# A convolution and a SiLU layer on one core: third product with x kept by token halves, and a new order with one run of each stage a block

## Chip, cores, metric

One core of one Trainium2 chip runs the whole program. The metric is device time in microseconds (us) of that core, the median of the runs shown; 2227.32 us for the kernel before (three runs, 2227.03 to 2227.95).

## What is computed

The reference, cut to what matters. A causal convolution with 7 taps along the tokens (24 channels share one set of taps, which come from a softmax), then two matrix products with SiLU between them, in fp32:

```
w = softmax(weight)                                  # [8 heads, 7 taps]
x_unf = x_pad[:, idx, :].reshape(B, S, K, H, group)  # x: [8, 4096, 192]
x = np.einsum('hk,bskhg->bshg', w, x_unf).reshape(32768, 192)
h = x @ w_in                                         # w_in: [192, 2048]
g = h * (1.0 / (1.0 + np.exp(-h)))
out = g @ w_out                                      # w_out: [2048, 192]
```

## The kernel before

The 32768 tokens go in 32 blocks (NB) of 1024 tokens (TT), each made of two halves of 512 (TB). The weights stay in SBUF.

**Stage h** computes x @ w_in. The 2048 columns are 4 groups j of 4 chunks c with 128 columns. Each pair (j, c) has two PSUM banks, h{j}{c}0 and h{j}{c}1, one for each half of the tokens. The 192 channels are split into 128 (tile xs[0], weights w_a) and 64 (tile xs[1], weights w_b, kept twice). Each operand has three versions, made by a split into a high part, a low part and a third one, so that three products in fp32r give fp32 accuracy. The function `up` issues all of it, by letters:

- A and C: versions 0 and 1, of w_a and of w_b. B and E: version 2, of w_a and of w_b.
- Every matmul uses 64 rows of TensorE. Two of them, e = 0 on the lower and e = 1 on the upper rows, stand next to each other and run together; one such couple is called a pair here. A.jc0, A.jc1 and C.jc are 2 pairs each, B.jc0, B.jc1 and E.jc one each: 9 pairs for every (j, c), 144 pairs a block.
- In C and E the row half e always writes bank e, since xs[1] and its weights are laid out by token halves. In A and B it writes bank e^n: with n = 1 the row halves write the banks the other way round.
- T.jc and U.jc read one column of bank 1 into `dot` on VectorE. They put a wait between a matmul of one row half into a bank and one of the other: T before A.jc1, U before B.jc1.
- X.jcn multiplies a bank by 1 + 1/4096 between the first two products and the third, on ScalarE. S.jcn is SiLU, from PSUM to the tile g, on ScalarE.

**Stage out** computes g @ w_out by a bilinear scheme that trades products for sums. Sums s0 to s12 of slots of g are made on VectorE, twice each (q = 0 for j 0 and 1, q = 1 for j 2 and 3). Twenty products Q.r.q (function `out_slot`, plain fp32) go into accumulators ob0 to ob8 in PSUM; the trace shows each fp32 matmul as two records of 256 columns, and two column halves run together. So there are 160 pairs of records in a block. The D tokens (`micro`) start the accumulators (Dz: zeros; Dk: a copy with a sign), combine them (Dh, Du on ScalarE, Di, Dj on VectorE) and transpose the results (DS); st stores.

**Preparation of x** for a later block: ld loads it to nat, i transposes it to xt, ha copies the halo, v.k0 to v.k6 are the seven taps (the first on ScalarE, the others on VectorE) and hx, lx, dx split it into versions 0, 1 and 2 of xs[k].

The string PLAN (lines 63 to 88) sets the order by hand for all engines at once. The tokens are issued in that order for each block; a sign ahead says which block is meant (- the one before, + the next, = two before, * two after). Every engine keeps its instructions in this order: PE, VectorE (DVE), ScalarE (ACT), GpSimd and the queue of SyncE (SP), from which the DMAs go. The helper that issues them is line 142, that of the matmuls line 475. PSUM banks go round in a list: a new user takes the bank that was given back longest ago. Block 0 is done apart, in plain fp32, beside the preparation of the weights.

Of the kernel before, what the change touches and what calls it, by code (L numbers as in the profile page):

```python
# [18 lines left out]
def kernel(  # L19
# [21 lines left out]
    P = 128  # L41
# [21 lines left out]
    PLAN = (  # L63
# [24 lines left out]
    )  # L88
# [41 lines left out]
    ON_DVE = (  # L130
        "Dk5.0", "Dz3.0",
    )
# [31 lines left out]
    for j in range(NJ):  # L164
        for c in range(4):
            touches.update({f"h{j}{c}0": 8, f"h{j}{c}1": 10})

# [16 lines left out]
    g_all = const.tile([P, 2, SLOTS, 2, TB], F32, name="g")  # L184
    fin = const.tile([P, 14, HT], F32, name="fin")

# [10 lines left out]
    xs = [const.tile([P, 3, n], F32R, name=f"xs{i}") for i, n in enumerate((TT, TB))]  # L197
    w_a = const.tile([P, 3, NJ, 4, P], F32R, name="w_a")
    w_b = const.tile([P, 3, NJ, 4, P], F32R, name="w_b")
    wd = const.tile([P, NJ, 20, R], F32, name="wd")  # L200
    ws = (w_a, w_b)

# [13 lines left out]
    NG = D // SQ  # L216
    w32 = const.tile([P, SQ], F32, name="w32")
    logits = w32[:, 0:K]
    wred = const.tile([P, 3], F32, name="wred")
    vec.memset(w32, 0.0)  # L220
# [11 lines left out]

    zeros = const.tile([P, P], F32, name="zeros")
    warm = const.tile([P, 1], F32, name="warm")
    vec.memset(zeros, 0.0)
    vec.memset(warm, 0.0)
    act.activation(warm, warm, AF.Exp)

    one_hot = const.tile([P, R], F32, name="hot")
    vec.memset(one_hot, 0.0)  # L240
# [56 lines left out]
    class Unit:  # L297


        def __init__(self, index, key, part):  # L300
            j = key[1]
            self.key, self.part, self.j, self.late = key, part, j, index > 0
            lo, hi = {0: (0, CA), 1: (CA, WC), None: (0, WC)}[part]
            n = hi - lo
            words = raw(key)[:, 2 * lo : 2 * hi]
            pairs = words.rearrange("p (c t) -> p c t", t=2)
            self.lo, self.hi = pairs[:, :, 0], pairs[:, :, 1]
            self.byte = words.bitcast(U8).rearrange("p (c t) -> p c t", t=8)[:, :, 0]
            at_ = scratch[:, 2 * WC * (index % 2) : 2 * WC * (index % 2) + 2 * WC]
            self.ex = at_[:, 0:n].bitcast(I32)  # L310
            self.mh = at_[:, n : 2 * n].bitcast(I32)
            if part is None:
                self.w = wd[:, j, 0:12, :].rearrange("p (a s) d -> p (a s d)", a=2)
                self.st = sticky_out.bitcast(I32)
            else:
                self.low = low_all[:, CA * part : CA * part + n]
                self.st = self.low.bitcast(I32)
            if part is not None:
                at_c = slice(0, 4) if part == 0 else slice(0, 2)
                self.to = [flat(ws[part][:, v, j, at_c, :]) for v in range(3)]  # L320
                self.w = flat(w_in[part][:, j, at_c, :])
# [39 lines left out]
        def split(self):  # L361
            vec.tensor_tensor(self.low, self.w, f32(self.to[0]), op=ALU.subtract)
            act.activation(self.to[1], self.low, AF.Copy, scale=SPLIT)
            vec.scalar_tensor_tensor(
                out=self.to[2], in0=f32(self.to[0]), scalar=1.0 / SPLIT, in1=self.low, op0=ALU.mult, op1=ALU.subtract
            )
            self.spread(f32(w_b[:, :, self.j, :, :]))

# [33 lines left out]
    taps = const.tile([P, 2, K], F32, name="taps")  # L402
    taps_all = const.tile([P, NG, SQ], F32, name="taps_all")
    turned = const.tile([P, SQ], F32, name="turned")
    by_channel = const.tile([P, D], F32, name="by_channel")
    top, total, part_ = (wred[:, i : i + 1] for i in range(3))
# [55 lines left out]
    def split(b, k, what):  # L462
        src = flat(nats[k])
        hi, lo, di = (xs[k][:, v, :] for v in range(3))
        if what == "h":
            act.activation(hi, src, AF.Copy, scale=BELOW)
        elif what == "l":
            vec.tensor_tensor(lo, src, f32(hi), op=ALU.subtract)
        else:
            vec.scalar_tensor_tensor(  # L470
                out=di, in0=f32(lo), scalar=SPLIT, in1=f32(hi), op0=ALU.mult, op1=ALU.subtract
            )

    def mm(to, lhs, rhs, start=False):
# [4 lines left out]
    def up(b, what, j, c, n=0):  # L479
        names = [f"h{j}{c}{i}" for i in range(2)]  # L480
        if what in "ABCE":
            fresh = (b, names[0]) not in held_at
            to = [at(b, name) for name in names]
            w, x_ = (w_a, xs[0]) if what in "AB" else (w_b, xs[1])
            for v in range(2) if what in "AC" else (2,):
                for e in range(2):
                    i = e ^ n
                    rhs = rows(x_, e)[:, v, ts(i, TB)] if what in "AB" else rows(x_, e)[:, v, :]
                    c_ = c if what in "AB" else (c + 2 * e) % 4
                    mm(to[i], rows(w, e)[:, v, j, c_, :], rhs, fresh and v == 0)  # L490
        elif what in "TU":
            vec.tensor_copy(dot, at(b, names[1])[:, 0:1])
# [12 lines left out]
    def micro(b, name):  # L505
# [19 lines left out]
        elif kind == "z":  # L525
            if on_dve:
                vec.memset(seen[to], 0.0)
            else:
                to_ = seen[to].rearrange("p (x c) -> p x c", x=2)
                act.copy(to_, zeros.unsqueeze(1).to_broadcast([P, 2, P]))  # L530
        elif kind == "t":
# [56 lines left out]
    def step(b, token):  # L588
# [9 lines left out]
        elif name in SUMS:  # L598
            sum_g(b, name, *digits)
        elif name in "ABCEXSTU":  # L600
            up(b, name, *digits)
# [8 lines left out]
        else:  # L610
            {"i": turn_in, "ha": halo_in, "v": conv}[name](b, *digits)

    base = {t.lstrip("-=+*") for t in plan}
    PREP = ("ld", "ha", "i", "v", "hx", "lx", "dx")
    prep = [t for t in base if t.split(".")[0] in PREP]
    did.update((0, t) for t in base if t[0] in "QDABCEXSTU" or t.split(".")[0] in (*SUMS, *PREP, "st"))

# [170 lines left out]
    for u in (2 * NJ + 2, 2 * NJ + 3):  # L788
        drain(work(u))
    for t in (*turns, *convs, "hx.0", "lx.0", "dx.0", "hx.1", "lx.1", "dx.1"):  # L790
        step(1, t)
# [25 lines left out]
    for b in range(1, NB + 3):  # L817
        for t in plan:
            if b == 2 and t[:2] == "-Q":
                drain(late)  # L820
            if b < NB or t[0] != "-" or t[1:].split(".")[0] not in AT_LAST:
                step(b, t)
            if b == 1 and t[0] in "TU":
                next(late, None)
# [46 lines left out]
```

## Time and profile before

| what | value |
|---|---|
| median of the runs | 2227.32 us (2227.03 to 2227.95) |
| the profiled execution | 2226.95 us, its span 2225.2 us |
| PE busy | 2215.2 us of the span |
| VectorE busy | 1827.8 us (82%) |
| ScalarE busy | 1288.0 us (58%) |
| granted TensorE clock | 1.0 over the whole span |
| matmuls of stage h, on xs and w_a | 5952 in 846.4 us, on w_b 2976 in 500.3 us |
| matmul records of stage out, 256 columns | 9920 in 1084.2 us |

Matmuls overlap, and their ends are modelled, so a busy PE doesn't show whether it is at its best. The starts of its instructions do: the time from the first matmul of a run to the first of the next run, over the pairs in it.

### The profile page before, as it was taken

The numbers are of one execution on the slowest core, as the hardware profiler recorded it, in microseconds if no ns is written. First come the engines' busy times: TensorE is split into PE (matmuls) and PEld (weight loads), VectorE is DVE, ScalarE is ACT, GpSimd is POOL, SyncE is SP. The second block draws the span as 40 slices with busy tenths as digits, with TensorE's granted clock in tenths as the row PEclk, the third lists the DMA queues.
The fourth block names the chain that finished last, engine by engine and source line by source line (L and its number), as shares of the span: only waits on it lengthen the run. The fifth ranks groups of instructions, "written<-read, shape, count | busy, mean of one in ns | idle before, by whom it ended". The sixth has DMA issues, their size and how long they took to land.

```text
span 2225.2 us, 47147 instructions
## 1 busy us (share of the span) xinstructions
PE 2215.2 (100%) x19294; PEld 1628.4 (73%) x19294; DVE 1827.8 (82%) x3035; ACT 1288.0 (58%) x2643; POOL 50.9 (2%) x73
## 2 busy tenths in 40 slices
PE   9999999999999999999999999999999999999998
PEld 4478777777777777777777777777777777777776
DVE  9897788877888877888778888788887788877877
ACT  5356655567555666555675546765456655567543
POOL 5300000000000000000000000000000000000000
PEclk9999999999999999999999999999999999999999
DMA  5301101111011110111110111101111101111001
GB/s 152 57 16 30 22 9 30 30 30 30 7 24 30 30 29 13 18 30 29 30 27 3 30 30 30 30 9 22 29 30 30 21 11 29 30 30 29 5 12 30
DMA packets 405737, 61.79 MB, mean 28 GB/s; under 512 B 400400, under 2 KB 404496, under 8 KB 405520
## 3 DMA queue, kind: packets, MB, share of 16 engines
q1 hardware_dynamic: 401200, 58.11, 15.1%
q8 instruction: 151, 2.47, 0.5%
q10 hardware_dynamic: 4320, 0.66, 0.2%
q14 instruction: 66, 0.54, 0.1%
HBM read 31.47 MB, written 25.17 MB: 25 GB/s over the span
## 4 chain that ended last, share of the span: by engine, by line
PE 98%; DVE 0%; SPq 0%; DMA 0%; issue 0%; ACT 0%; ACTq 0%; DVEq 0%
PE ps L475 98%; DVE nat L142 0%; SPq L142 0%; DMA nat<-in_x_dram 0%; DMA fin<-in_moe_w_in_dram 0%; DMA w<-in_weight_dram 0%; DVE fin L142 0%; DVE dot L142 0%; ACT ps L142 0%; DVE w L142 0%; DVE g L142 0%; DVE wd L142 0%; DVE wred L142 0%; ACTq L142 0%; DVE zeros L142 0%
## 5 line engine op out<-in xcount | busy, mean ns | idle before, releaser
L475 PE MATMUL ps<-g,wd 128*64 128x256 f32 (+1 forms) x10112 | 1125.6, 384 | 0.0
L475 PEld LDWEIGHTS ps<-g,wd 128*64 128x64 f32 x10112 | 720.4, 137 | 395.7 <-issue 35.1
L142 DVE TENSOR_TENSOR g<-g 128x1024 f32<-128x1024 f32 x806 | 951.4, 1219 | 9.1 <-PE ps L475 5.5
L475 PE MATMUL ps<-xs,w_a 64*128 64x512 f32 x5952 | 846.4, 390 | 0.9 <-DVE dot L142 0.7
L142 ACT ACTIVATE ps<-ps 128x512 f32<-128x512 f32 (+1 forms) x1085 | 567.9, 581 | 297.6 <-PE ps L475 249.7
L475 PEld LDWEIGHTS ps<-xs,w_a 64*128 64x128 f32 x5952 | 590.8, 184 | 109.5 <-DVE dot L142 14.4
L142 ACT ACTIVATE g<-ps 128x512 f32<-128x512 f32 x1024 | 559.8, 616 | 58.1 <-PE ps L475 49.4
L475 PE MATMUL ps<-xs,w_b 64*128 64x512 f32 x2976 | 500.3, 391 | 0.0
L142 DVE COPY dot<-ps 128x1 f32<-128x1 f32 x992 | 155.6, 157 | 355.6 <-PE ps L475 346.3
L142 DVE SCALAR_TENSOR_TENSOR nat<-xt,taps,nat 128x512 f32<-128x512 f32 (+1 forms) x378 | 374.1, 1003 | 1.9 <-ACT nat L142 1.4
L475 PEld LDWEIGHTS ps<-xs,w_b 64*128 64x128 f32 x2976 | 300.9, 184 | 54.2 <-issue 11.5
L142 ACT COPY fin<-ps 128x256 f32<-128x256 f32 (+1 forms) x127 | 47.6, 376 | 404.9 <-PE ps L475 404.9
L142 DVE TENSOR_TENSOR fin<-fin,ps 128x256 f32<-128x256 f32 x248 | 95.9, 405 | 17.1 <-PE ps L475 17.1
L142 DVE STREAM_TRANSPOSE fin<-fin 128x256 f32<-128x256 f32 (+1 forms) x189 | 83.4, 442 | 1.2
L142 ACT ACTIVATE nat<-xt,taps 128x512 f32<-128x512 f32 (+1 forms) x63 | 58.6, 933 | 16.1 <-DVE xt L142 14.7
L142 DVE STREAM_TRANSPOSE xt<-nat 128x1024 f32<-128x1024 f32 (+3 forms) x67 | 61.9, 928 | 0.0
L142 DVE SCALAR_TENSOR_TENSOR xs<-xs 128x1024 fp32r<-128x1024 f32 (+1 forms) x62 | 58.9, 950 | 0.1
L142 DVE TENSOR_TENSOR xs<-nat,xs 128x1024 fp32r<-128x1024 f32 (+1 forms) x62 | 58.9, 951 | 0.0
L142 ACT ACTIVATE xs<-nat 128x1024 fp32r<-128x1024 f32 (+1 forms) x62 | 52.6, 848 | 10.9 <-DVE nat L142 10.9
L142 ACT ACTIVATE fin<-ps 128x256 f32<-128x256 f32 x93 | 35.8, 385 | 39.4 <-PE ps L475 38.0
L142 ACT COPY xt<-xt 64x6 f32<-64x6 f32 x58 | 11.3, 195 | 64.8 <-DVE xt L142 64.2
L475 PE MATMUL ps<-nat,wd 128*128 128x512 f32 (+1 forms) x128 | 44.0, 601 | 1.5 <-DMA g<-in_moe_w_in_dram 1.3
(57 smaller groups left out, 254.0 us busy)
## 6 DMA issues: line engine op xcount, KB each, us to landing
out_dram<-fin SPq DMA_DIRECT2D x242, 96.0 KB, 2.4
nat<-in_x_dram SPq DMA_DIRECT2D x124, 128.0 KB, 2.9
nat<-in_x_dram SPq DMA_DIRECT2D x131, 64.0 KB, 2.4
g<-in_moe_w_in_dram SPq DMA_DIRECT2D x12, 128.0 KB, 3.2
fin<-in_moe_w_in_dram SPq DMA_DIRECT2D x12, 128.0 KB, 3.1
g<-in_moe_w_out_dram SPq DMA_DIRECT2D x2, 768.0 KB, 4.9
w_b<-w_b SPq DMA_DIRECT2D x8, 192.0 KB, 4.7
fin<-in_moe_w_out_dram SPq DMA_DIRECT2D x2, 768.0 KB, 5.0
```

Of the source, the lines that this page charges most:

```text
L142: return lambda *args, **kw: pin(getattr(self.engine, name)(*args, **kw))
L475: return pin(nc.tensor.matmul(to, lhs, rhs, start=start, stop=True, skip_group_check=True))
```

## The change

**The third product.** Version 2 of the first 128 channels of x gets a layout of its own, xd: row half e holds token half e, and the two channel halves lie one behind the other in the free dimension (index o; o = 0 are the half's own channels, o = 1 those of the other half). `split` therefore writes version 2 into nats[0], and the new function `move_d` (token dm.0) copies it to xd in four DMAs of 64 rows by 512. Version 2 of w_a is now the tile w_d, which has each row half's own channels and, copied by two DMAs a group j in the setup, those of the other half. Both B matmuls of a pair now write bank e for either n, as C and E do. The tokens U are gone with their 16 reads a block.

**The order.** PLAN is new. Stage h and stage out stand in one run each a block. X.301, X.311, X.321, X.331, Dz0 and Dz1 go from ScalarE to VectorE. The small tiles of the setup (w32, wred, zeros, warm, one_hot, taps_all, turned, by_channel) lie now inside g, in a part that block 0 writes later; fin has 13 slots instead of 14.

```
     ON_DVE = (
-        "Dk5.0", "Dz3.0",
+        "Dk5.0", "Dz3.0", "Dz0.0", "Dz1.0", "X.301", "X.311", "X.321", "X.331",
     )
...
-            touches.update({f"h{j}{c}0": 8, f"h{j}{c}1": 10})
+            touches.update({f"h{j}{c}0": 8, f"h{j}{c}1": 9})
...
+    xd = xs[0][:, 2, :].rearrange("p (o t) -> p o t", o=2)
+    w_a = const.tile([P, 2, NJ, 4, P], F32R, name="w_a")
+    w_d = const.tile([P, 2, NJ, 4, P], F32R, name="w_d")
...
+            if self.part == 0:
+                for e in range(2):
+                    own, other = (f32(rows(w_d, r)[:, o, self.j]) for r, o in ((1 - e, 0), (e, 1)))
+                    sync.dma_start(out=other, in_=own)
...
-                out=di, in0=f32(lo), scalar=SPLIT, in1=f32(hi), op0=ALU.mult, op1=ALU.subtract
+                out=di if k else src, in0=f32(lo), scalar=SPLIT, in1=f32(hi), op0=ALU.mult, op1=ALU.subtract
...
+    def move_d(b, k):
+        for e in range(2):
+            for o in range(2):
+                of = rows(flat(nats[k]), e ^ o)[:, ts(e, TB)]
+                sync.dma_start(out=f32(rows(xd, e)[:, o, :]), in_=of)
...
-                    i = e ^ n
-                    rhs = rows(x_, e)[:, v, ts(i, TB)] if what in "AB" else rows(x_, e)[:, v, :]
-                    c_ = c if what in "AB" else (c + 2 * e) % 4
-                    mm(to[i], rows(w, e)[:, v, j, c_, :], rhs, fresh and v == 0)
-        elif what in "TU":
+                    if what == "A":
+                        i = e ^ n
+                        w, x_ = w_a[:, v, j, c, :], xs[0][:, v, ts(i, TB)]
+                    elif what == "B":
+                        i, w, x_ = e, w_d[:, n, j, c, :], xd[:, n, :]
+                    else:
+                        i, w, x_ = e, w_b[:, v, j, (c + 2 * e) % 4, :], xs[1][:, v, :]
+                    mm(to[i], rows(w, e), rows(x_, e), fresh and v == 0)
+        elif what == "T":
...
-            if on_dve:
-                vec.memset(seen[to], 0.0)
-            else:
-                to_ = seen[to].rearrange("p (x c) -> p x c", x=2)
-                act.copy(to_, zeros.unsqueeze(1).to_broadcast([P, 2, P]))
+            vec.memset(seen[to], 0.0)
```

Of PLAN's text a piece tells little; the end of its last line is shown, which closes stage h, and the start of the first, which opens stage out of the block before:

```
-        "-U.30 -X.321 -B.301 -C.33 -X.320 -U.31 -s2.0 -A.330 -S.301 -T.33 -E.32 -Dz0.0 hx.1  "
+        "-Q0.0 lx.0 -Dz3.0 -S.331 -Q13.0 dx.0 -Q13.1 -S.310 -Dk15.0 -s2.1 dm.0 -Q0.1 -Q11.1  "
...
-        "-DS16.0 E.30 A.321 S.231 S.230 B.310 E.31"
+        "E.33 B.330"
```

**On PE, at the boundary of two blocks.** The rows are those of the programs; xs_75 is xs[0], xs_76 is xs[1], g with wd is stage out, and xN counts equal instructions in a row (an fp32 matmul of stage out is one instruction here, 160 a block). Before:

```order
L475 MATMUL ps<-xs_75,w_a 128x512 x10
L475 MATMUL ps<-g,wd 64x256 x16
L475 MATMUL ps<-xs_76,w_b 128x512 x4
L475 MATMUL ps<-xs_75,w_a 128x512 x6
L475 MATMUL ps<-xs_76,w_b 128x512 x2
L475 MATMUL ps<-xs_75,w_a 128x512 x6
L475 MATMUL ps<-g,wd 64x256 x144
L475 MATMUL ps<-xs_75,w_a 128x512 x4
```

The same place in the program of the change, where line 495 is the matmul's helper:

```order
L495 MATMUL ps<-xs_76,w_b 128x512 x4
L495 MATMUL ps<-xs_75,w_d 128x512 x4
L495 MATMUL ps<-xs_76,w_b 128x512 x2
L495 MATMUL ps<-xs_75,w_d 128x512 x2
L495 MATMUL ps<-g,wd 64x256 x160
L495 MATMUL ps<-xs_76,w_b 128x512 x4
L495 MATMUL ps<-xs_75,w_a 128x512 x8
```

Before, 4 products of stage out (16 matmuls) are followed by 18 matmuls of stage h and then by the other 144; now the 160 stand together, and so do the 288 of stage h.

**On VectorE, where stage h ends and stage out begins.** In the change (xs_75 and nat_71 belong to the 128 channels, xs_76 and nat_73 to the 64; TENSOR_TENSOR g<-g is a sum s, TENSOR_SCALAR on ps an X, the memsets Dz):

```order
L141 TENSOR_SCALAR ps<-ps 128x512
L141 COPY dot<-ps 128x1
L141 TENSOR_SCALAR ps<-ps 128x512 x2
L141 TENSOR_TENSOR xs_76<-nat_73,xs_76 128x512
L141 MEMSET ps 128x256 x2
L141 TENSOR_TENSOR g<-g 128x1024
L141 TENSOR_TENSOR xs_75<-nat_71,xs_75 128x1024
L141 MEMSET ps 128x256
L141 SCALAR_TENSOR_TENSOR nat_71<-xs_75 128x1024
L141 TENSOR_TENSOR g<-g 128x1024 x10
```

The same piece before:

```order
L142 TENSOR_TENSOR g<-g 128x1024
L142 TENSOR_TENSOR xs_76<-nat_73,xs_76 128x512
L142 TENSOR_TENSOR g<-g 128x1024
L142 TENSOR_TENSOR xs_75<-nat_71,xs_75 128x1024
L142 TENSOR_TENSOR g<-g 128x1024
L142 COPY dot<-ps 128x1 x2
L142 TENSOR_TENSOR g<-g 128x1024
L142 MEMSET ps 128x256
L142 TENSOR_TENSOR g<-g 128x1024 x11
L142 COPY ps<-ps 128x256
```

Now the last three X (after T.32: X.311, then T.33, X.321 and X.331), lx.1, Dz0 and Dz1 stand ahead of s1.1, the only sum between the end of h's X and lx.0, Dz3 and dx.0. Before, the sums s0.0, s1.1 and s4.0 stood around the splits lx.1 and lx.0, then came two reads, s2.1 and Dz3, and dx.0 came only after 14 more sums.

More of the change, by code (lines that the diff above doesn't have):

```diff
@@ L184 @@
     g_all = const.tile([P, 2, SLOTS, 2, TB], F32, name="g")
-    fin = const.tile([P, 14, HT], F32, name="fin")
+    fin = const.tile([P, 13, HT], F32, name="fin")
     ORDER = (0, 2, 1, 3)
@@ L197 @@
     xs = [const.tile([P, 3, n], F32R, name=f"xs{i}") for i, n in enumerate((TT, TB))]
-    w_a = const.tile([P, 3, NJ, 4, P], F32R, name="w_a")
+    xd = xs[0][:, 2, :].rearrange("p (o t) -> p o t", o=2)
+    w_a = const.tile([P, 2, NJ, 4, P], F32R, name="w_a")
+    w_d = const.tile([P, 2, NJ, 4, P], F32R, name="w_d")
     w_b = const.tile([P, 3, NJ, 4, P], F32R, name="w_b")
     wd = const.tile([P, NJ, 20, R], F32, name="wd")
-    ws = (w_a, w_b)
+    ws = [[w_a[:, 0], w_a[:, 1], w_d[:, 0]], [w_b[:, v] for v in range(3)]]
     def g_slot(j, c, n):
@@ L216, with early @@
     NG = D // SQ
-    w32 = const.tile([P, SQ], F32, name="w32")
+    room = flat(g_all[:, 0, 0])
+    used = [0]
+    def early(n):
+        used[0] += n
+        return room[:, used[0] - n : used[0]]
+    w32 = early(SQ)
     logits = w32[:, 0:K]
-    wred = const.tile([P, 3], F32, name="wred")
+    wred = early(3)
     vec.memset(w32, 0.0)
@@ L231 @@
         load_first(i, False, act if i % 2 else sync)
-    zeros = const.tile([P, P], F32, name="zeros")
-    warm = const.tile([P, 1], F32, name="warm")
+    zeros = early(P)
+    warm = early(1)
     vec.memset(zeros, 0.0)
@@ L237 @@
     act.activation(warm, warm, AF.Exp)
-    one_hot = const.tile([P, R], F32, name="hot")
+    one_hot = early(R)
     vec.memset(one_hot, 0.0)
@@ L319, in __init__ @@
                 at_c = slice(0, 4) if part == 0 else slice(0, 2)
-                self.to = [flat(ws[part][:, v, j, at_c, :]) for v in range(3)]
+                self.to = [flat(w[:, j, at_c, :]) for w in ws[part]]
                 self.w = flat(w_in[part][:, j, at_c, :])
@@ L402 @@
     taps = const.tile([P, 2, K], F32, name="taps")
-    taps_all = const.tile([P, NG, SQ], F32, name="taps_all")
-    turned = const.tile([P, SQ], F32, name="turned")
-    by_channel = const.tile([P, D], F32, name="by_channel")
+    taps_all = early(NG * SQ).rearrange("p (g i) -> p g i", g=NG)
+    turned = early(SQ)
+    by_channel = early(D)
     top, total, part_ = (wred[:, i : i + 1] for i in range(3))
@@ L483, in up @@
             to = [at(b, name) for name in names]
-            w, x_ = (w_a, xs[0]) if what in "AB" else (w_b, xs[1])
             for v in range(2) if what in "AC" else (2,):
                 for e in range(2):
-                    i = e ^ n
-                    rhs = rows(x_, e)[:, v, ts(i, TB)] if what in "AB" else rows(x_, e)[:, v, :]
-                    c_ = c if what in "AB" else (c + 2 * e) % 4
-                    mm(to[i], rows(w, e)[:, v, j, c_, :], rhs, fresh and v == 0)
-        elif what in "TU":
+                    if what == "A":
[7 more added lines that the diff above has]
+        elif what == "T":
             vec.tensor_copy(dot, at(b, names[1])[:, 0:1])
@@ L599, in step @@
             sum_g(b, name, *digits)
-        elif name in "ABCEXSTU":
+        elif name in "ABCEXST":
             up(b, name, *digits)
@@ L610, in step @@
         else:
-            {"i": turn_in, "ha": halo_in, "v": conv}[name](b, *digits)
+            {"i": turn_in, "ha": halo_in, "v": conv, "dm": move_d}[name](b, *digits)
     base = {t.lstrip("-=+*") for t in plan}
-    PREP = ("ld", "ha", "i", "v", "hx", "lx", "dx")
+    PREP = ("ld", "ha", "i", "v", "hx", "lx", "dx", "dm")
     prep = [t for t in base if t.split(".")[0] in PREP]
-    did.update((0, t) for t in base if t[0] in "QDABCEXSTU" or t.split(".")[0] in (*SUMS, *PREP, "st"))
+    did.update((0, t) for t in base if t[0] in "QDABCEXST" or t.split(".")[0] in (*SUMS, *PREP, "st"))
     units = [Unit(2 * j + i, ("i", j), i) for j in range(NJ) for i in range(2)]
@@ L789 @@
         drain(work(u))
-    for t in (*turns, *convs, "hx.0", "lx.0", "dx.0", "hx.1", "lx.1", "dx.1"):
+    for t in (*turns, *convs, "hx.0", "lx.0", "dx.0", "dm.0", "hx.1", "lx.1", "dx.1"):
         step(1, t)
@@ L822 @@
                 step(b, t)
-            if b == 1 and t[0] in "TU":
+            if b == 1 and t[0] in "TE":
                 next(late, None)
```

43 rows, old and new, of the table PLAN are left out of this document.

## The prediction

> **What bounds the kernel now.** First the page's busy times and its chain of work that ended last.
>
> ```profile
> PE 2215.2 (100%) x19294; PEld 1628.4 (73%) x19294; DVE 1827.8 (82%) x3035; ACT 1288.0 (58%) x2643; POOL 50.9 (2%) x73
> ...
> PE 98%; DVE 0%; SPq 0%; DMA 0%; issue 0%; ACT 0%; ACTq 0%; DVEq 0%
> ```
>
> PE is never without work, and 98% of the chain is PE. So only what PE's own stream costs can change the time: the number of its instructions, their pace, and what is lost between them. The number stays the same. For the pace I read PE's timeline over one block in the middle (start, length, instructions), taking starts only, since the ends are modelled.
>
> ```profile
> 1020.68 1.32 PE L475 MATMUL ps<-xs,w_a 64*128 64x512 f32 x10
> 1021.93 3.67 PE L475 MATMUL ps<-g,wd 128*64 128x256 f32 x32
> 1025.54 0.73 PE L475 MATMUL ps<-xs,w_b 64*128 64x512 f32 x4
> 1026.11 0.90 PE L475 MATMUL ps<-xs,w_a 64*128 64x512 f32 x6
> 1026.85 0.40 PE L475 MATMUL ps<-xs,w_b 64*128 64x512 f32 x2
> 1027.08 0.92 PE L475 MATMUL ps<-xs,w_a 64*128 64x512 f32 x6
> 1027.93 31.30 PE L475 MATMUL ps<-g,wd 128*64 128x256 f32 x288
> 1059.16 0.73 PE L475 MATMUL ps<-xs,w_a 64*128 64x512 f32 x4
> ...
> 1090.22 3.67 PE L475 MATMUL ps<-g,wd 128*64 128x256 f32 x32
> ```
>
> A block is four runs: 16 pairs of stage out (1021.93 to 1025.54: 3.61 us), 9 pairs of stage h (to 1027.93: 2.39 us), 144 pairs of out (to 1059.16: 31.23 us) and 135 pairs of h (to 1090.22: 31.06 us). Together 68.29 us.
>
> A long and a short run of each kind tell a price per pair from a price per run. Stage out: (31.23 - 3.61) / (144 - 16) = 0.2158 us a pair, and 3.61 - 16 x 0.2158 = **0.16 us a run**. Stage h: (31.06 - 2.39) / (135 - 9) = 0.2275 us a pair, and 2.39 - 9 x 0.2275 = **0.34 us a run**. The reader sees the same in the row at 1025.54: its 2 pairs take 0.57 us to the next row, where 0.46 would do, and the last start before it is late too. Whether the 0.34 is all a price of the turn from one stage to the other, or holds waits of this short run, the rows don't part.
>
> **What the others do beside it.** The windows of a long out run and of a long h run (PE, PEld, DVE, ACT, POOL busy, with their instructions):
>
> ```profile
> 1028.00:1059.00 31.00, 31.00 (x288) 20.51 (x288) 30.45 (x35) 7.52 (x17) 0.00 (x0) 1.00 0.17 28
> 990.00:1022.00 32.00, 32.00 (x282) 26.88 (x280) 21.09 (x54) 28.55 (x57) 0.20 (x2) 1.00 0.07 12
> ```
>
> VectorE is full beside stage out (30.45 of 31 us) and ScalarE nearly beside stage h (28.55 of 32 us), and still PE runs at its pace. Either is one step from being the bound.
>
> **The change, part by part.** *One run of each stage.* Blocks 1 to 31 each have one out run and one h run less. The 25 pairs of the short runs go on at the pace of the long ones. That removes 0.16 + 0.34 = 0.50 us a block; the block becomes 0.16 + 160 x 0.2158 = 34.69 for out and 0.34 + 144 x 0.2275 = 33.10 for h, 67.79 us. Over 31 blocks: **-15.5 us**. In the last block the short run was worse:
>
> ```profile
> 2186.51 0.50 PE L475 MATMUL ps<-xs,w_a 64*128 64x512 f32 x2
> 2186.85 0.40 PE L475 MATMUL ps<-xs,w_b 64*128 64x512 f32 x2
> 2187.50 0.50 PE L475 MATMUL ps<-xs,w_a 64*128 64x512 f32 x2 [0.26 <-DVE dot L142]
> 2187.93 31.30 PE L475 MATMUL ps<-g,wd 128*64 128x256 f32 x288
> ```
>
> 3 pairs took 1.42 us, 0.74 more than 3 x 0.2275, so 0.4 more goes there. The Trainium skill, "TensorEngine Tiling (Array Packing)", Key Properties, says that a change of tiling mode drains TensorE, and "TensorE: Matmul & The Clock Gate", Single matmul latency, gives a lone matmul a constant of 166 ns at full clock. Two turns of the mode (64 rows by 128 columns, 128 by 64) would by that cost an estimated 0.33 us, 10 us over 31 blocks, and the time would be 2217; the rows agree that each turn costs, but give 0.50.
>
> *Layout of the third product.* B has as many matmuls, of the same shape. Its U reads go:
>
> ```profile
> L142 DVE COPY dot<-ps 128x1 f32<-128x1 f32 x992 | 155.6, 157 | 355.6 <-PE ps L475 346.3
> PEld ps L475 <- DVE dot L142: 14.4, 65, 0.7
> ```
>
> Half of 992 reads at 0.157 us are 2.5 us a block of VectorE, in stage h where it has idle time (21.09 of 32 us busy): nothing by itself. The weight loads waited 14.4 us in all for such reads; at most half, 7 us, could come on top, and at least nothing, since the loads run ahead of the matmuls. I take nothing, and keep 5 us for the range.
>
> *Moves to VectorE.* The rows that price them:
>
> ```profile
> L142 ACT ACTIVATE ps<-ps 128x512 f32<-128x512 f32 x992 | 536.7, 601 | 100.0 <-PE ps L475 98.4
> L142 DVE COPY ps<-ps 128x256 f32<-128x256 f32 x31 | 13.2, 425 | 0.0
> L142 DVE TENSOR_TENSOR g<-g 128x1024 f32<-128x1024 f32 x806 | 951.4, 1219 | 9.1 <-PE ps L475 5.5 <-ACT g L142 0.3
> L142 DVE TENSOR_TENSOR xs<-nat,xs 128x512 fp32r<-128x512 f32 x31 | 21.2, 684 | 0.0
> L142 DVE MEMSET ps<- 128x256 f32 x31 | 8.4, 272 | 1.6
> L142 ACT ACTIVATE g<-ps 128x512 f32<-128x512 f32 x1024 | 559.8, 616 | 58.1 <-PE ps L475 49.4
> ```
>
> No row shows X on VectorE. The copy in PSUM of half the width takes 0.425 us, so it lies between that and 0.85; with the slope of the two sums, (1219 - 684) / 512 = 1.04 ns a column, 0.425 + 256 x 1.04 ns = 0.69 us, which I take. Four of them and two zeros are 3.3 us more a block on VectorE; with the 2.5 less it is nearly even. ScalarE loses 4 x 0.60 and two copies. What matters is the place: X.331, lx.1, Dz0, Dz1 and s1.1 stand ahead of the third product of stage out. From the end of A.331 to Q13.1 PE has 10 pairs of h (2.28 us), the turn (0.16) and 8 pairs of out (1.73): 4.2 us. VectorE needs 0.69 + 0.68 + 0.54 + 1.22 = 3.1; but Dz1 takes a bank from S.321, which needs E.32 (5 pairs, 1.1 us), then 0.62 for S.321, 0.27 and 1.22: 3.3. **0.9 us are left**, less a few tenths for signals. At the upper end for X, 0.85, it is 3.3 on the other way too, so nothing changes.
>
> *VectorE through stage out.* Its pace from the timeline:
>
> ```profile
> 1029.06 12.83 DVE L142 TENSOR_TENSOR g<-g 128x1024 f32<-128x1024 f32 x11 [0.15 <-PE ps L475]
> 1041.80 0.42 DVE L142 COPY ps<-ps 128x256 f32<-128x256 f32 x1
> 1042.14 3.61 DVE L142 TENSOR_TENSOR g<-g 128x1024 f32<-128x1024 f32 x3
> 1045.66 1.22 DVE L142 SCALAR_TENSOR_TENSOR xs<-xs 128x1024 fp32r<-128x1024 f32 x1
> 1046.80 0.41 DVE L142 TENSOR_TENSOR fin<-fin,ps 128x256 f32<-128x256 f32 x1
> 1047.13 4.62 DVE L142 TENSOR_TENSOR g<-g 128x1024 f32<-128x1024 f32 x4
> ```
>
> A sum takes (1041.80 - 1029.06) / 11 = 1.158 us from start to start, other work of 1024 columns 1.14, of 256 columns 0.33. From the end of s1.1 (0.8 us into stage out) to the first read T.00 of the next h it has 23 sums (26.6), three pieces of 1024 (3.4), two of 512 (1.4), the memset, Dk5 and six combinations (2.6): 34.0 us beside PE's 34.7. In order, s2.1 ends 4.5 us into the run, Q16.1 starts at 6.2 (a product takes 4 x 0.2158 = 0.863); s4.0 6.8, Q19.0 7.9; s10.0 18.7, Q12.0 20.0; s11.1 32.7 (after 0.6 of wait for Q12.1), Q4.1 33.8. **The least margin is 1.1 us**, so no wait on PE here. At the start of h, Di14_9 gives the bank of C.02 back at about 37.3, and C.02 comes 14 pairs after the turn, at 38.1.
>
> *DMAs.* SP gets dm.0, four copies, ahead of the loads of the next x:
>
> ```profile
> nat<-in_x_dram SPq DMA_DIRECT2D x131, 64.0 KB, 2.4
> w_b<-w_b SPq DMA_DIRECT2D x8, 192.0 KB, 4.7
> ```
>
> They wait for dx.0 (3.4 us into stage out), so 128 KB land, between these rows, by about 8 us; the first B.001 comes 30 us later. The loads behind them on SP are due at i.1 (22 us into the run) and i.0. All hidden: free, unless DMAs were late by over 10 us. The eight copies of w_d in the setup follow the weights' split on SP, beside PE's work; I take 0, and 2 us for the range.
>
> Sum: 2226.95 - 15.5 - 0.4 = 2211.1 for the profiled execution (span 2225.2 with 1.75 around it). The median of the runs is 0.4 above that execution: **2211.5 us**.
>
> **The rivals.** *New waits at the turns.* The 0.34 of an h run may be partly waits, and as much may come back in the long run, where T, X and SiLU stand closer. Half of the gain lost, 0.25 us a block, gives 2219; the margins of 0.8 and 0.9 speak against it, their small size for it. *ScalarE becomes the bound of h (slower).* Each of 12 pairs of banks in h waits for two SiLUs. ScalarE had 53 X and S in the 31.06 us of the long run and has 55 in 33.1: as dense as before, with nothing to spare, in a new order. From 0.042 us of wait at each of the 12 places the gain is gone (0.50 us a block), from 0.054 it is slower by 4.5 us; at 0.08 it is 0.96 - 0.50 = 0.46 us a block, 14 us in all, 2241. *The change doesn't do what it says*: the price is not the turn's but that of waits which move along, so 0 to 4 us are gained, 2223 to 2227. *The reads set h's pace.* If h's 0.2275 came from waits for reads and went down to out's 0.2158, 144 x 0.0117 = 1.7 us a block more would go: 2159. Against it: T stays, and E and C, ahead of which no read stands, are in the same mean. The Trainium skill, "TensorE: Matmul & The Clock Gate", Back-to-back issue gap, gives 216 ns for 512 columns; by that rule 2159 would be possible, but only out's rows agree with it.
>
> **How the numbers follow.** A difference under 0.2% (4.5 us) can't be told from none. Forecast, 2206 to 2217: 0.63. New waits, 2217 to 2222.9: 0.17. Pace of h: 0.03. Nothing gained: 0.10. Slower by ScalarE: 0.07. Faster 0.83, same 0.10, slower 0.07. The range 2206 to 2223 holds the first two, 0.80, with the 5 us of the reads below and the 2 us of the setup.
>
> **What the profile after would show.** Two runs a block on PE, of 288 and 320 matmuls, 33.1 and 34.7 us from start to start, a period of 67.8. Waits of PE or of its weight loads for VectorE at the third product, or for SiLU at the new banks, would show the rivals; so would an h run over 33.6. Pairs at 0.216 in h would prove the fourth. A first h run that starts later than before would show a dearer setup.

## The result, and the profile after

| kernel | median us | lowest to highest | ratio to before, 95% interval |
|---|---|---|---|
| before | 2227.39 | 2227.03 to 2227.95 | |
| the change | 2210.05 | 2209.53 to 2211.5 | 0.9923 (0.9906 to 0.994) |

The change is 17.3 us faster, 0.8%. The forecast was 2211.5. The profiled execution took 2210.07 us, its span is 2208.3 (before 2225.2). The busy times and the chain that ended last, on its page:

```profile
PE 2194.7 (99%) x19294; PEld 1586.5 (72%) x19294; DVE 1870.8 (85%) x2725; ACT 1219.1 (55%) x2457; POOL 50.5 (2%) x73
...
PE 94%; DVE 1%; SPq 0%; DMA 0%; issue 0%; ACT 0%; DVEq 0%; ACTq 0%
```

PE still holds the chain, and its count of matmuls is the same. Its share of the chain fell from 98% to 94%, so somewhere PE now waits. First PE's timeline over one block in the middle (start, length, instructions):

```profile
1016.86 34.75 PE L495 MATMUL ps<-g,wd 128*64 128x256 f32 x320
1051.54 0.73 PE L495 MATMUL ps<-xs,w_b 64*128 64x512 f32 x4
...
1084.09 0.39 PE L495 MATMUL ps<-xs,w_d 64*128 64x512 f32 x2
1084.41 34.75 PE L495 MATMUL ps<-g,wd 128*64 128x256 f32 x320
1119.09 0.73 PE L495 MATMUL ps<-xs,w_b 64*128 64x512 f32 x4
```

Two runs a block: out from 1016.86 to 1051.54, 34.68 us, and h from there to 1084.41, 32.87. In the usual block (the median of the 29 between the first and the last two), the period went from 68.28 to **67.547 us: 0.737 a block less**, where 0.50 was forecast. The mean of before is 68.30, as some of its blocks took about 0.1 longer, so the 29 blocks together gained 21.9 us. Out came as forecast (34.69). In h, 33.45 us (31.06 + 2.39) became 32.86, where 33.10 was forecast.

The windows of an out run and of an h run, columns as before:

```profile
1085.00:1118.00 33.00, 33.00 (x310) 21.96 (x308) 32.38 (x35) 7.90 (x20) 0.00 (x0) 1.00 0.37 66
1052.00:1084.00 32.00, 32.00 (x286) 26.43 (x284) 22.93 (x46) 28.93 (x57) 0.19 (x1) 1.00 0.00 1
```

VectorE is full beside out and ScalarE nearly full beside h, as before, and PE has no gap in either.

**Where the rest went.** The two ends lost most of what the middle won beyond the forecast:

| piece of the span | before | after | difference | forecast |
|---|---|---|---|---|
| start to the first h | 99.61 | 99.63 | 0.0 | 0 |
| first h to second h | 71.50 | 73.81 | +2.3 | -0.5 |
| the 29 blocks between | 1980.74 | 1958.86 | -21.9 | -14.5 |
| last h to the end | 73.35 | 76.01 | +2.7 | -0.9 |

The outer two pieces are not quite like for like. Before, the first held 150 pairs of h and the last 138; now both hold 144. Six pairs are 1.36 us at h's pace of 0.2267. For the same work, then, the first block came out 4.2 us behind the forecast (2.3 + 1.36 + 0.5) and the last 2.2 us (2.7 - 1.36 + 0.9).

*The first block*, on PE:

```profile
99.63 0.73 PE L495 MATMUL ps<-xs,w_b 64*128 64x512 f32 x4
...
101.12 0.62 PE L495 MATMUL ps<-xs,w_b 64*128 64x512 f32 x4
104.78 0.73 PE L495 MATMUL ps<-xs,w_a 64*128 64x512 f32 x4 [3.03 <-DVE dot L141]
```

PE waits 3.03 us for a read T. VectorE was not busy; its own row just ahead of that read shows what it waited for:

```profile
102.02 1.25 DVE L141 STREAM_TRANSPOSE xt<-nat 128x1024 f32<-128x1024 f32 x1 [4.87 <-DMA nat<-in_x_dram]
```

This is i.0 for the next block, and T.00 stands behind it. It waited for loads that were issued late. SP's rows, of the change and then of before:

```profile
92.92 2.40 SPq L141 DMA_DIRECT2D xs<-nat  x4
97.08 4.87 SPq L141 DMA_DIRECT2D nat<-in_x_dram  x8
```

```profile
91.63 4.75 SPq L142 DMA_DIRECT2D nat<-in_x_dram  x8
```

The four copies dm.0 stand ahead, and the loads overwrite the tile that these copies read: they went out 5.4 us later than before. Then something follows from PE's wait. A window three microseconds long, of the change and of before:

```profile
106.00:109.00 3.00, 3.00 (x15) 2.11 (x13) 2.15 (x5) 3.00 (x6) 0.00 (x0) 0.50 0.37 63
```

```profile
106.00:109.00 3.00, 3.00 (x28) 2.37 (x28) 1.88 (x8) 3.00 (x7) 0.00 (x0) 1.00 0.73 126
```

The granted clock is 0.50 instead of 1.00, and PE issues 15 matmuls instead of 28. This lasts from 105.82 to 109.23, 3.41 us. It doesn't follow that half of that time was lost: experiment 11 shows the same stretch of work at full clock, and it is no faster.

*The last block*, on PE:

```profile
2165.15 31.30 PE L495 MATMUL ps<-g,wd 128*64 128x256 f32 x288
2198.62 3.67 PE L495 MATMUL ps<-g,wd 128*64 128x256 f32 x32 [2.17 <-DVE ps L141]
```

Only the last block's order puts Dj9 and some other tokens at the end, in before too, where PE's row shows no wait. Now Q4.0 waits for Dj9, which stands on VectorE behind three sums, an addition and a transposition of results. What comes after PE's last matmul did not grow: 5.98 us to the end of the span, 5.92 before.

### The profile page after: what moved, and what is told of

It is laid out like the page before. It is cut to its first block, busy times and chain, and to the rows that moved or that the text cites. A ratio compares the mean times of both kernels' runs of the same rounds, so it can differ in the third digit from the quotient of the medians.

```text
span 2208.3 us, 46344 instructions
## 1 busy us (share of the span) xinstructions
PE 2194.7 (99%) x19294; PEld 1586.5 (72%) x19294; DVE 1870.8 (85%) x2725; ACT 1219.1 (55%) x2457; POOL 50.5 (2%) x73
## 4 chain that ended last, share of the span: by engine, by line
PE 94%; DVE 1%; SPq 0%; DMA 0%; issue 0%; ACT 0%; DVEq 0%; ACTq 0%
PE ps L495 94%; DVE nat L141 1%; DVE g L141 0%; SPq L141 0%; DVE xt L141 0%; DMA nat<-in_x_dram 0%; DVE fin L141 0%; DMA xs<-nat 0%; DVE wd L141 0%; ACT nat L141 0%; DVE xs L141 0%; DVEq L141 0%; DVE ps L141 0%; DVE dot L141 0%; ACTq L141 0%
## 5 line engine op out<-in xcount | busy, mean ns | idle before, releaser
L141 DVE TENSOR_TENSOR g<-g 128x1024 f32<-128x1024 f32 (+1 forms) x813 | 947.9, 1211 | 21.0 <-PE ps L495 11.6
L141 ACT ACTIVATE ps<-ps 128x512 f32<-128x512 f32 (+1 forms) x961 | 499.0, 579 | 421.2 <-PE ps L495 387.0
L495 PE MATMUL ps<-xs,w_a 64*128 64x512 f32 x3968 | 568.0, 387 | 3.5 <-DVE dot L141 3.5
L495 PE MATMUL ps<-xs,w_b 64*128 64x512 f32 x2976 | 489.4, 389 | 0.0
L495 PEld LDWEIGHTS ps<-xs,w_a 64*128 64x128 f32 x3968 | 372.8, 184 | 83.0 <-DVE dot L141 5.0
L495 PEld LDWEIGHTS ps<-xs,w_b 64*128 64x128 f32 x2976 | 278.1, 184 | 68.9 <-issue 12.3
L495 PE MATMUL ps<-xs,w_d 64*128 64x512 f32 x1984 | 321.4, 386 | 0.0
L141 DVE COPY dot<-ps 128x1 f32<-128x1 f32 x496 | 78.3, 158 | 247.0 <-PE ps L495 238.3
L495 PEld LDWEIGHTS ps<-xs,w_d 64*128 64x128 f32 x1984 | 186.7, 184 | 38.6
L141 DVE TENSOR_SCALAR ps<-ps 128x512 f32<-128x512 f32 x124 | 86.5, 697 | 34.7 <-PE ps L495 34.7
```

What stands on the lines that cost most here:

```text
L141: return lambda *args, **kw: pin(getattr(self.engine, name)(*args, **kw))
L495: return pin(nc.tensor.matmul(to, lhs, rhs, start=start, stop=True, skip_group_check=True))
```

## Experiments

Each kernel is after with the edit shown, if nothing else is said. Every ratio is against runs of before on the same chip (2227.25 to 2228.15 us). The theory was that a turn from one shape of matmul to the other costs a fixed time, and that one turn there and back was taken out of each block. Its rival was that only waits were moved.

**1. split_runs: one short run of h put back.** C.00 and A.000 (4 pairs) go ahead of the last four products of out, so h and out stand in two runs each again.

```
-  ... dx.1 -Q4.0 -Q17.0 -Di16_11.0 -Q17.1 +ha.2 +i.0 -Q5.1 -Di14_f.0 -Q4.1 C.00 A.000 -Di12_9.0 ...
+  ... dx.1 -Q4.0 C.00 A.000 -Q17.0 -Di16_11.0 -Q17.1 +ha.2 +i.0 -Q5.1 -Di14_f.0 -Q4.1 -Di12_9.0 ...
```

> The kernel of the change, with C.00 and A.000 (4 pairs of stage h) moved ahead of the last four products of stage out (Q17.0, Q17.1, Q5.1, Q4.1): four runs a block again, nothing else changed. If the turn from one stage to the other has a price of its own, the block of 67.55 us grows by 0.36 to 0.50 us and the time by 11 to 15 us, to 2221 to 2225. If only waits for reads, SiLUs or sums cost, and the turn is free, the time stays within 2 us of 2210.

Measured: 2222.74 us (2221.32 to 2225.3), ratio 0.998 (0.9971 to 0.999). PE over a block:

```profile
1024.45 31.30 PE L495 MATMUL ps<-g,wd 128*64 128x256 f32 x288
1055.68 0.73 PE L495 MATMUL ps<-xs,w_b 64*128 64x512 f32 x4
1056.25 0.62 PE L495 MATMUL ps<-xs,w_a 64*128 64x512 f32 x4
1056.81 3.67 PE L495 MATMUL ps<-g,wd 128*64 128x256 f32 x32
1060.41 0.73 PE L495 MATMUL ps<-xs,w_a 64*128 64x512 f32 x4
...
1092.37 31.30 PE L495 MATMUL ps<-g,wd 128*64 128x256 f32 x288
```

The period is 67.92 (1092.37 - 1024.45), in the mean 0.380 more than without the split. No row has a wait in brackets. Pair by pair, the trace puts the price right at the turns: the last pair of out takes 0.10 us longer than the others and the first 0.05, the first pair of h 0.11 and the last 0.09 to 0.10. The runs of the change show the same, and before's out runs and first pairs of h. The 4 pairs take 1.13 us, 0.22 more than at the pace of h; the 16 pairs of out 3.60, 0.15 more than at the pace of out.

**2. split_twice: two short runs.** Is it a price per turn? C.00 goes ahead of Q17.0 and A.000 ahead of Q5.1, so there are two turns there and back more than in the change.

```
-  ... -Q4.0 -Q17.0 ... +i.0 -Q5.1 -Di14_f.0 -Q4.1 C.00 A.000 -Di12_9.0 ...
+  ... -Q4.0 C.00 -Q17.0 ... +i.0 A.000 -Q5.1 -Di14_f.0 -Q4.1 -Di12_9.0 ...
```

> The kernel of the change, with C.00 (2 pairs) ahead of Q17.0 and A.000 (2 pairs) ahead of Q5.1: six runs a block. If every run that is added costs the same, whatever its length and place, the block grows by twice the 0.38 us of split_runs, to 68.31 us, and the time by 23 us, to 2233 or so. If the price hangs on the length of the pieces or on what waits there, the block grows by less than 0.6 or more than 0.9.

Measured: 2234.14 us (2232.64 to 2235.07), ratio 1.0026 (1.0014 to 1.0038). PE:

```profile
1026.85 31.30 PE L495 MATMUL ps<-g,wd 128*64 128x256 f32 x288
1058.08 0.73 PE L495 MATMUL ps<-xs,w_b 64*128 64x512 f32 x4
1058.74 1.95 PE L495 MATMUL ps<-g,wd 128*64 128x256 f32 x16
...
1095.16 31.30 PE L495 MATMUL ps<-g,wd 128*64 128x256 f32 x288
```

68.31 a block, 0.763 more than in the change: twice 0.38. The price belongs to the turn. The first two pairs of h, from 1058.08 to 1058.74, take 0.66 us for 0.45 of work. So of the 0.737 gained a block 0.380 is the turn, and 0.357 is something else.

**3. layout_alone: the new layout with the old order.** Before's PLAN without the tokens U, with dx.0 and dm.0 set earlier, and X on ScalarE again.

```
-        "Dk5.0", "Dz3.0", "Dz0.0", "Dz1.0", "X.301", "X.311", "X.321", "X.331",
+        "Dk5.0", "Dz3.0",
...
-        "-U.30 -X.321 -B.301 ...          (before's PLAN)
+        "-X.321 -B.301 ... -Q0.1 -s6.0 dx.0 dm.0 +ld.1 ...
```

> The kernel of the change with the order of before (four runs a block, all X on ScalarE): U dropped, dx.0 and dm.0 moved ahead of the first load into the tile that dx.0 now writes. If turns make the gain, the block stays at 68.0 to 68.3 us and the time at 2220 to 2230, the first block's wait included. If the reads made it, the block falls to 67.8 or less and the time under 2217.

Measured: 2235.85 us (2235.33 to 2238.12), ratio 1.0041 (1.0026 to 1.0056).

```profile
1028.87 3.67 PE L495 MATMUL ps<-g,wd 128*64 128x256 f32 x32
...
1034.81 31.52 PE L495 MATMUL ps<-g,wd 128*64 128x256 f32 x288
...
1097.33 3.67 PE L495 MATMUL ps<-g,wd 128*64 128x256 f32 x32
```

In the usual block the short h run is 0.05 us shorter than before and the long one 0.01 longer; the long out run is 0.21 longer: PE has gaps at Q3.0 and Q7.0, whose sums now stand on VectorE behind the earlier dx.0. Without 16 reads a block h gains at most 0.05 us. Taking the reads away is no gain of its own worth speaking of.

**4. order_alone: the new order with the old layout.** Before's code and layout with the new PLAN, the tokens U put in, and each B.jc1 about three tokens later, so that it need not follow its read at once.

```
-        "-U.30 -X.321 -B.301 ...          (before's PLAN)
+        "-Q0.0 lx.0 -Dz3.0 -S.331 ... X.001 E.00 B.000 U.00 X.010 X.011 A.030 +v.11 T.02 A.021 B.010 B.001 ...
```

> The kernel before (old layout, U reads, no copies to xd) with the new order: one run of each stage a block, the same X and Dz on VectorE; where the old layout forbids it, B.jc1 goes behind U.jc and some three PE tokens later than B.jc0. If the order alone makes the gain, the block is 67.5 to 67.8 us and the time 2206 to 2212, as the first block has no copies to wait for. If the layout is what lets PE run on, B.jc1 waits for its read at many places, the h run is over 33.3 us, and the time over 2216.

Measured: 2554.23 us (2549.14 to 2557.97), ratio 1.1467 (1.145 to 1.1484). Out stays at 34.68, h takes about 43.6. The waits of PE (total, times, longest):

```profile
PEld ps L475 <- DVE dot L142: 249.8, 247, 2.1
PE ps L475 <- DVE dot L142: 147.0, 185, 1.7
```

In this form the order can't run with the old layout: h waits for the reads U.

**5. reads_back: the change with the reads put back.** B writes bank e for either n and needs no read; here one stands ahead of the later matmul of each bank couple all the same.

```
-  ... E.00 B.001 B.000 ...
+  ... E.00 B.001 U.00 B.000 ...
```

> The kernel of the change, with the 16 U reads a block back in VectorE's stream, each ahead of the last third product of its pair of banks (the new layout doesn't need them). If the runs' turns made the gain, the time stays within 2 us of 2210. If the reads cost, which is the rival for the 0.24 us a block that came on top of the forecast, the h run goes from 32.86 to about 33.1 us and the time to about 2217.

Measured: 2548.54 us (2547.6 to 2551.23), ratio 1.1446 (1.1427 to 1.1466).

```profile
PEld ps L496 <- DVE dot L142: 354.2, 468, 3.4
PE ps L496 <- DVE dot L142: 162.2, 372, 3.0
```

Neither expectation had this. In most blocks h takes 43.05 to 43.11 us, 10.2 more, or 0.64 for each of the 16 reads; in the others half the clock was granted for 3.41 us, and it takes 44.4 to 44.7. The placement is the cost: the read waits for a matmul just issued, and the next one stands right behind the read. It says nothing on reads with room around them.

**6. reads_late: the same reads where no matmul waits for them**, between the two SiLUs of a couple.

```
-  ... S.000 S.001 ...
+  ... S.000 U.00 S.001 ...
```

> The kernel of the change, with the 16 U reads a block put where nothing on PE has to wait for them soon, between the two SiLUs of their pair of banks. If a read costs only by the matmul that waits behind it, the h run stays under 33.0 us and the time within 3 us of 2210. If the reads' time on VectorE or the bank given back late costs, the h run grows by 0.2 us or more and the time to 2216 or beyond.

Measured: 2297.47 us (2296.11 to 2298.45), ratio 1.0312 (1.0296 to 1.0327); h 34.9, out 35.36.

```profile
ACT g L142 <- DVE dot L142: 119.1, 155, 1.6
```

Now ScalarE waits for the read, and the bank comes free late. In both kernels a read cost what stood behind it, not its 0.16 us on VectorE.

**7. x_on_act: the four X back on ScalarE.**

```
-        "Dk5.0", "Dz3.0", "Dz0.0", "Dz1.0", "X.301", "X.311", "X.321", "X.331",
+        "Dk5.0", "Dz3.0", "Dz0.0", "Dz1.0",
```

> The kernel of the change with X.301, X.311, X.321, X.331 back on ScalarE. If ScalarE has room at the end of stage h, the h run grows by under 0.1 us a block and the time by at most 3 us. If ScalarE is one step from being the bound there, as the rival of the prediction had it, S.321 and s1.1 come 1 to 2 us later, PE waits at the last third products and at Q13.1, and the block grows by 0.5 us or more: 2225 or beyond.

Measured: 2239.33 us (2238.65 to 2239.66), ratio 1.0053 (1.0038 to 1.0068): slower than before.

```profile
1031.10 34.75 PE L495 MATMUL ps<-g,wd 128*64 128x256 f32 x320
...
1099.58 34.75 PE L495 MATMUL ps<-g,wd 128*64 128x256 f32 x320
```

The period is 68.48, 0.93 more than in the change; out is the same, h 33.80. PE loses time at the end of h: 0.20 us at B.310, 0.11 at A.331, 0.23 at B.331, 0.11 at E.33, and 0.32 at B.330, of which 0.09 is the turn. The second matmuls of B.310 and of B.331 start 0.04 us after ScalarE's X.311 and X.331. The waits of the weight loads for ScalarE's X came up, from 0.2 us in the change:

```profile
PEld ps L495 <- ACT ps L141: 29.0, 61, 0.5
```

**8. before_x_on_dve: the same four X moved to VectorE, in before.**

```
-        "Dk5.0", "Dz3.0",
+        "Dk5.0", "Dz3.0", "X.301", "X.311", "X.321", "X.331",
```

> The kernel before, with X.301, X.311, X.321, X.331 moved to VectorE and nothing else. If ScalarE's lateness at the end of stage h is what PE's waits of 0.1 to 0.2 us a block around the short runs come from, the block falls from 68.28 to 68.1 or less and the time by 4 to 8 us. If VectorE, full beside stage out in that order, can't take 2.8 us more, its sums come late and the time grows, to 2240 or more.

Measured: 2230.93 us (2230.21 to 2233.01), ratio 1.0012 (1.0002 to 1.0021). The usual block takes 68.42 us, 0.13 more, of which 0.10 is in the short h run. In the old order the move gains nothing; it loses a little, far less than was thought possible.

**9. aside: dx.0 of block 1 into another tile.** So that the first loads need not wait for dm.0's reads, the third version goes into slots of fin that are still unused.

```
+    aside = flat(fin[:, 0:4])
...
-                out=di if k else src, ...
+                out=di if k else aside if b == 1 else src, ...
...
-                of = rows(flat(nats[k]), e ^ o)[:, ts(e, TB)]
+                of = rows(aside if b == 1 else flat(nats[k]), e ^ o)[:, ts(e, TB)]
```

> The kernel of the change, but for block 1 alone dx.0 writes version 2 into a free part of fin instead of nats[0], and dm.0 copies it from there, so that the loads of block 2 need not wait for the four copies. If that wait made the first h run 39.1 us long, it falls by 2.5 to 3 us and the time to about 2207. If the run is long for the other work that VectorE has there (combining w_out's weights, storing block 0), it falls by less than 0.5 us.

Measured: 2211.1 us (2210.03 to 2212.69), ratio 0.9924 (0.9908 to 0.9941). A miss. The loads still stood behind dm.0 in SP's queue and went out at 96.10; PE waited 1.65 us, and the clock fell all the same. The first h run took 38.26 instead of 39.12. In this profile the wait at the end was followed by the half clock too:

```profile
2199.00:2201.00 2.00, 2.00 (x14) 1.06 (x12) 0.96 (x3) 0.00 (x0) 0.00 (x0) 0.50 0.48 80
```

**10. dj9_early: Dj9 in its usual place in the last block.**

```
-    AT_LAST = "Dj9 Q4 Di16_11 ...
+    AT_LAST = "Q4 Di16_11 ...
```

> The kernel of the change, with Dj9 of the last block left in its place in the order instead of behind all else. If the wait of 2.17 us ahead of Q4 in the last block is Dj9's place behind s0.1, s5.1, s11.1 and DS15, it goes but for a few tenths (Q4.1 then waits for s11.1), and the time is about 2208. If s11.1 is what Q4 waits for anyway, nothing changes.

Measured: 2210.96 us (2209.46 to 2212.66), ratio 0.9924 (0.9909 to 0.9939).

```profile
2198.92 2.81 PE L495 MATMUL ps<-g,wd 128*64 128x256 f32 x24 [0.62 <-DVE g L141]
```

The wait went from 2.17 to 0.62 and the last out run from 36.77 to 35.22. From its start to the end of the span only 0.7 us were gained (43.15 to 42.46): from PE's last matmul to the end it is now 6.84 us instead of 5.98. There VectorE's last results and the stores set the end.

**11. both_ends: 9 and 10 together.**

```
+    aside = flat(fin[:, 0:4])
...
-    AT_LAST = "Dj9 Q4 Di16_11 ...
+    AT_LAST = "Q4 Di16_11 ...
```

> Both edits to the first and the last block together. If the two losses are apart, about 4.5 us less than the change's 2210: 2205 to 2206.

Measured: 2208.61 us (2207.9 to 2210.07), ratio 0.9914 (0.9899 to 0.9929), less of a gain than expected. The first h run took 37.97.

This profile also tells what the half clock cost. The first block is edited as in 9, and PE waited 1.92 us, but the clock stayed at 1.00 throughout. PE, ScalarE and the window as above:

```profile
104.06 0.20 ACT L141 COPY xt<-xt 64x6 f32<-64x6 f32 x1 [12.23 <-DVE dot L141]
...
104.12 0.73 PE L497 MATMUL ps<-xs,w_a 64*128 64x512 f32 x4 [1.92 <-DVE dot L141]
...
107.38 2.06 ACT L141 ACTIVATE ps<-ps 128x512 f32<-128x512 f32 x4
108.04 0.98 PE L497 MATMUL ps<-xs,w_b 64*128 64x512 f32 x2 [0.67 <-ACT ps L141]
```

```profile
106.00:109.00 3.00, 2.33 (x17) 1.44 (x16) 2.23 (x6) 3.00 (x6) 0.00 (x0) 1.00 0.54 93
```

PE issues 17 matmuls here at full clock, 15 in the change at half. From the matmul that waited to the out run it took 33.95 us, in the change 33.98 (138.75 - 104.78), in 9 34.50. The late loads hold up ScalarE too: its halo copy waits for i.1 (to 104.02; the row names the read just behind it), three copies and two taps follow, and the first X starts 3.3 us after PE goes on, in the change as well. So in the change the half clock cost next to nothing on top of that, and in 9 at most 0.55.

**12. loads_first** adds to 11 what 9 had missed: the next block's loads stand ahead of dm.0 on SP in the setup.

```
-    for t in (*turns, *convs, "hx.0", "lx.0", "dx.0", "dm.0", "hx.1", "lx.1", "dx.1"):
+    for t in (*turns, *convs, "hx.0", "lx.0"):
         step(1, t)
+    for t in ("ld.0", "ld.1", "ld.2", "ld.3"):
+        step(2, t)
+    for t in ("dx.0", "hx.1", "lx.1"):
+        step(1, t)
+    for t in ("ld.4", "ld.5", "ld.6", "ld.7"):
+        step(2, t)
+    for t in ("dm.0", "dx.1"):
+        step(1, t)
```

> Both edits to the ends, and for block 1 the eight loads of block 2 now stand ahead of the four copies dm.0 on SP. If those copies' place in SP's queue is what still holds the first h run at 38.0 us, i.0 of block 2 waits no more for its loads, the run falls to 36.2 to 36.6 us with the clock at 1.0 all through, and the time to about 2207. If the run's other work on VectorE holds it, it stays at 37.5 or more and the time at 2208.6.

Measured: **2204.75 us** (2204.03 to 2205.31), ratio 0.9899 (0.9883 to 0.9916), a larger gain than expected. SP's rows and the window of the first h run:

```profile
91.32 4.61 SPq L141 DMA_DIRECT2D nat<-in_x_dram  x8
95.97 2.41 SPq L141 DMA_DIRECT2D xs<-fin  x4
```

```profile
106.00:109.00 3.00, 3.00 (x30) 2.48 (x28) 2.64 (x6) 2.96 (x7) 0.00 (x0) 1.00 0.68 117
```

The loads go out at 91.32, as in before; the clock is 1.00, and the first h run takes 33.67 us, 5.45 less than in the change. Of that, 3.20 lie ahead of the matmul that waited (5.15 us from the run's start, now 1.95), and 2.25 behind it (33.98, now 31.72). There the first X on ScalarE starts 0.7 us after that matmul and not 3.3. This is the fastest version of all.

## Why the prediction was right, and where it was not

The sign and the number held, 2210.05 against 2211.5, and the mechanism for about half of the gain. The number is partly luck, because two misses balance: the middle gained 7.4 us more than forecast, the ends 6.4 less.

**One run of each stage, "0.50 us a block": right in kind, mis-sized.** Measured 0.737. The part that belongs to the turn is 0.380 (experiments 1 and 2, which agree with each other within 0.01). The step took 0.34 for an h run from a long and a short run of before, and said that it might hold waits. It does: with 0.22 for the turn and h's pace of 0.2267 us a pair ((32.86 - 0.22) / 144), the short run of before held 2.39 - 9 x 0.2267 - 0.22 = 0.13 us of waits. What the step couldn't see is that the long run held some too, 31.06 - 135 x 0.2267 - 0.22 = 0.24, since a difference of two runs that both wait puts the waits into the pace (0.2275). In the trace 0.09 of the 0.24 is one pair near the run's end, the rest some twenty pairs that are 4 to 10 ns late; that all of it is waits is a reading, as no row marks one. Out, which had no waits, came to 34.68 against 34.69.

**Which part of the change took the 0.36 of waits away is only half settled.** The layout alone takes at most 0.05 (experiment 3), moving X alone none (8). The new order with the old layout loses 10 us a block (4), with X on ScalarE 0.93 (7). In the arrangements tried, then, it takes all three together; how the 0.36 divides was not found.

**The price of a turn.** 0.38 us there and back, though nobody waits. The rule of the Trainium skill that a change of tiling mode drains TensorE ("TensorEngine Tiling (Array Packing)", Key Properties) is in line with that, though no run shows a drain as such; the estimate of 0.33 from its lone-matmul constant was near.

**Layout, "I take nothing": right.** 0.05 us a block is 1.6 us, within the 5 kept for the range.

**Moves to VectorE, "nothing": right as a price, wrong as a weighing.** X took 0.697 us where 0.69 was worked out, and s1.1 ran to 1.1 us into out, where 0.8 was expected; no wait came of it. The group, and VectorE at the turn (out starts at 1084.41):

```profile
L141 DVE TENSOR_SCALAR ps<-ps 128x512 f32<-128x512 f32 x124 | 86.5, 697 | 34.7 <-PE ps L495 34.7
```

```profile
1084.11 0.27 DVE L141 MEMSET ps<- 128x256 f32 x1 [0.25 <-ACT g L141]
1084.29 1.21 DVE L141 TENSOR_TENSOR g<-g 128x1024 f32<-128x1024 f32 x1
```

But these four moves are what keeps the rival "ScalarE becomes the bound of h" away. Without them h takes 0.93 more a block and the kernel is slower than before (experiment 7), near the 2241 that the rival had, but by another way: it had 0.08 us of wait at each of 12 places, and the trace has the waits behind two X at the end of h. The prediction counted ScalarE's instructions, 55 in the run, and gave the rival 0.07 without seeing that the moves decide it.

**DMAs, "All hidden": wrong in the first block.** The step looked at a block in the middle, where the loads are due 22 us later. In the setup dm.0 and the loads stand close together, and the loads waited for the tile. For the same work the first block came out 4.2 us behind the forecast; experiment 12 took back 5.45.

**The last block, "0.4 more": wrong.** The short run and its waits went, but a wait of 2.17 us for Dj9 came, for which the step had not looked. For the same work the block came out 2.2 us behind the forecast, which is this wait. Experiment 10 took 1.55 us of it away and yet brought only 0.7, since the work behind PE then set the end.

**The other rivals.** Waits at the turns did not come. "Nothing gained" falls with experiments 1 and 2. "The reads set h's pace" falls: the pairs stay at 0.2267 with half of the reads gone, and did not go to 0.2158. Where the Trainium skill, "TensorE: Matmul & The Clock Gate", Back-to-back issue gap, gives about 216 ns for an isolated matmul of 512 columns (and 131 ns in a sustained stream), h's pairs take 226.7 ns, and the measurement decides. Out's 0.2158 us, which the prediction set beside that figure, is for pairs of 256 columns.

## What to carry over

Price the steady block from its own runs, but check every run for waits first: a slope between two runs that both wait hides them in the pace. Then walk through the first and the last block by themselves, queue by queue, because a copy that is hidden by 22 us in the middle may stand right ahead of a load at the start. And ask of every move "what if it were not made": the four moves that were costed at nothing held a gain larger than the whole one. Where two losses stand one behind the other, look for a profile that has the first without the second before both are added up.

## What the runs showed of the hardware

- **A turn between 64 x 128 and 128 x 64 costs TensorE 0.38 us there and back**, with no wait in the rows, and twice that for two (experiments 1 and 2).
- **After a short wait of PE the granted clock can fall to 0.50 for 3.41 us.** It did after 3.03 us of idle PE in the change. What that costs hangs on what bounds PE: next to nothing here (experiment 11), but in reads_back, out runs with such a stretch in them took 36.35 to 36.37 us instead of 34.68. Within one profile these stretches begin whole multiples of 3.413 us apart: 105.82 and 2205.01 in the change, 106.24, 2198.61 and 2208.85 in aside. The Trainium skill, "TensorE: Matmul & The Clock Gate", Part 1, tells of a free-running window of 3413 ns and of half rate after an idle one. The length and the grid agree; but waits shorter than a window were enough here, 1.65 us in the first block of aside and 2.16 in its last. The 2.16 lies within one window of the grid (2195.20 to 2198.61); the 2.17 in the change's last block, after which the clock stayed, is cut by the grid at 2198.19 into 1.74 and 0.43. How much of a window must be idle these runs don't settle: of aside's 1.65 only 1.28 lie in one window.
- **A read that orders two matmuls costs what stands behind it**: 0.16 us on VectorE, 0.64 on PE when the matmul follows at once (experiment 5).
